# Turned attention probabilities kept in DRAM in another order: four stores a unit for two, one load for four

## The chip, the cores and the metric

The kernel runs on one core of a Trainium2 chip. The metric is the device time of one execution in microseconds (us), the median of several runs. The core has a matrix engine (PE, with its weight loads shown as PEld), a vector engine (DVE), a scalar engine (ACT), a general engine (POOL), and SP, which computes nothing and only issues transfers (DMAs). Each engine works through its own list of instructions in order and waits on semaphores. Transfers are issued here by SP and by ACT and are moved by 16 DMA engines that both share.

## The reference

Sparse causal attention over 8 batches, 8 heads, 576 positions and 64 features, followed by a feed-forward layer over all 4608 tokens. All of it is float32.

```python
scores = scale * np.matmul(q, k.transpose(0, 1, 3, 2))
rel = pos[:, None] - pos[None, :]
mask_local = (rel >= 0) & (rel < stride)                    # stride 32, heads 0 to 3
mask_strided = (rel >= 0) & (pos[None, :] % stride == pos[:, None] % stride)   # heads 4 to 7
...
attn = np.exp(scores)
attn = attn / (np.sum(attn, axis=-1, keepdims=True) + 1e-09)
return np.matmul(attn, v).astype(np.float32)
...
h = x @ w_in                                                # 4608x512 by 512x2048
g = np.where(pos, h, np.where(neg, 0.0, (h + beta) ** 2 / (4.0 * beta)))
return (g @ w_out).astype(np.float32)                       # 4608x2048 by 2048x512
```

## The kernel before

**Two kinds of work share PE.** The feed-forward layer is most of it: nine chunks of 512 tokens. The first three are computed plainly (`up`, L775, and `down`, L820, 16 slices of the hidden layer each). The other six are taken in three pairs by a scheme with seven products for eight (`up_block`, L917, and `down_block`, L1005). Each float32 operand is split into two rounded parts, so a product takes three matmuls. The weights of the seven-product part are sums of weight blocks that are kept in DRAM (`kq`, `ks`). SP fetches them with `fetch_w` (L845) into a ring of seven tiles `wr`: as soon as PE is done with one tile, the transfer for the tile seven places later may go.

**Attention feeds the layer.** A batch is four units: 0 and 1 hold the local heads, 2 and 3 the strided heads. Units 0 and 2 have n = 6 slots, unit 1 has 3 and unit 3 has 5. A slot holds, on 128 partitions, four groups of 32 queries, against 64 keys for each of two heads. For each unit: scores on PE (L482), mask, maximum, exponential, sum and division on DVE, ACT and POOL, then the turn of the probabilities from "query on the partitions" to "key on the partitions", and last the value step on PE (`value`, L669), which multiplies them with V into `xp`. Its result is copied into the feed-forward input.

**The turn has two forms.** Batches 0 and 1 turn on PE (`flip`, `keep`). Batches 2 to 7, that is 24 units, do it in three steps. `turn` (L633) transposes 32x32 blocks on DVE, into two tiles `t`, one for each head h, whose partition is (group i, key c within its half) and whose row is (half of the keys k, slot n, query q). `spread` (L643) stores the two tiles to a DRAM tile `there`. `gather` (L654) loads it back into `pT`, whose partition is (head h, half k, key c) and whose row is (group i, slot n, query q), which is what the value step reads. PE runs the value steps of units 1 and 3 of a batch together (`values_1_3`).

**What sets the order.** All is issued in an order written out by hand: the table `WORK` gives each step of each unit a place between the matmul groups of the feed-forward layer (`s` scores, `t` turn, `j` spread, `J` gather, `v` and `V` value). SP's list holds, in that order, the loads of q, k and v, the stores and loads of `there`, the fetches of `wr`, and the output. A load of `there` waits until the stores have landed, and SP issues nothing behind it until then. SP's transfers take turns on eight semaphores; a transfer whose semaphore is still in use waits for the one that uses it.

The turn and the two steps that the change touches:

Of the kernel before, what the change touches and what calls it, by code (L numbers as in the profile page):

```python
# [8 lines left out]
F32 = mybir.dt.float32  # L9
# [8 lines left out]
P = 128  # L18
EPS = 1e-09
ST = 32  # L20
# [153 lines left out]
def tile_sparse_attention_then_ffn(  # L174
# [14 lines left out]
    nc = tc.nc  # L189
    B, _, _, _, S = qk_l.shape  # L190
# [27 lines left out]
    def slots(u):  # L218

        n, rest = divmod(UNITS[u][2], IL if UNITS[u][0] else IS)  # L220
        return n + (rest > 0), n
# [18 lines left out]
    dram = ctx.enter_context(tc.tile_pool(name="dram", bufs=1, space=bass.MemoryType.DRAM))  # L240
# [31 lines left out]
    for i in range(IL):  # L272
        part = slice(i * QL, (i + 1) * QL)
        for n0, n1, off in ((0, SLOTS, ST),) if i else ((0, 1, 0), (1, SLOTS, ST)):
            t = m_loc[part, n0:n1]
# [4 lines left out]
    for i in range(IS):  # L280
        t = m_str[i * QS:(i + 1) * QS]
# [164 lines left out]
    def attention(b, kinds):  # L446

        probs, flipped, there, ahead, covered = {}, {}, {}, {}, set()
# [188 lines left out]
        def spread(u):  # L637

            ts = probs.pop(u)
            n = sum(slots(u))  # L640
            there[u] = to = dram.tile([P, 2, 2, n, ST], F32, tag=f"t{u}", name=f"there_{b}_{u}")
            for h in range(2):
                nc.sync.dma_start(to[:, h], ts[h][:, :, :n])  # L643

        def gather(u):

            n = sum(slots(u))
            pool, tag = (o_p, "ob") if u == 1 else (pt_p, "pT")
            pT = pool.tile([P, 4, n if u == 1 else 2 * SLOTS, ST], F32, tag=tag, name=f"pT_{b}_{u}")
            src = there.pop(u).rearrange("(i c) h k n q -> h k c i (n q)", c=ST)  # L650
            for h in range(2):
                for k in range(2):
                    at = h * 64 + k * ST
                    nc.sync.dma_start(pT[at:at + ST, :, :n].rearrange("p i n q -> p i (n q)"), src[h, k])  # L654
            flipped[u] = pT

        def value(u, xp=None):
# [85 lines left out]
        def in_two(do, rest):  # L743

            return lambda u: do(u, rest if b == 0 else None)

        steps = {"s": score, "y": score_0, "z": score_1, "m": mask, "o": opened, "i": cover, "g": plain, "X": most_there, "S": below_there, "x": most, "w": norm_v, "a": below_max, "e": expo, "q": total, "p": plus_eps, "k": plus_eps_v, "b": below_max_v, "r": norm,
                 "f": flip, "t": turn, "j": spread, "J": gather, "c": keep, "d": keep_v, "v": value, "V": values_1_3, "h": in_two(high, False), "l": in_two(low, False), "H": in_two(high, True), "M": in_two(low, True),
                 "Q": lambda p: fetch_qk(b, p), "P": lambda n: last_weights(n), "F": lambda n: fetch_v(b, ((0, 0), (0, 1), (1, 0), (2, 0), (3, 0))[n])}
        def go(names):  # L750
# [292 lines left out]
    with tc.manual_schedule():  # L1043
# [33 lines left out]
        for s, work in G_WORK.items():  # L1077
            for t, name in work:
                m, k = int(name[1]), int(name[2:])
# [13 lines left out]
        for c in range(CLASSIC):  # L1093
            for f in range(NF):
                t = 4 * (NF * (c - 1) + f)
# [17 lines left out]
        for s in range(NSC):  # L1113
            t = 4 * NF * (CLASSIC - 1) + 2 * len(UP) * s
# [61 lines left out]
```

## Time and profile before

| | us |
|---|---|
| median of three runs | 816.55 (816.5 to 817.0) |
| the profiled execution | 817.29 |
| its span | 815.5 |
| PE busy | 806.2 |
| DVE, ACT, POOL busy | 574.7, 495.4, 232.5 |

The profile is of one execution. Its span runs from the first to the last instruction; the execution's own time also holds what lies around it, 1.8 us. A page gives the busy time of each engine, the DMA queues (q1 is SP's, q10 is ACT's) and the chain of work that ended last, followed back from the end. Rows of a timeline give start, length, engine, line, operation, what is written from what, and how often. Rows on DMA issues give how many, the size of each, and the median time from issue to landing. In the trace the three plain chunks end at about 328 us, the first store of `there` is issued at 135.6 us and the last load of it at 559 us.

### The profile page before, as it was taken

How to read it: one execution, taken by the hardware profiler on the slowest of the kernel's cores; microseconds unless marked ns; L12 is line 12 of the kernel's file. 1: busy time of each engine (PE TensorE's matmuls, PEld its weight loads, DVE VectorE, ACT ScalarE, POOL GpSimd, SP SyncE). 2: the span in 40 equal slices, each digit the busy share in tenths (PEclk: the TensorE clock that was granted, in tenths of full speed). 3: DMA queues.
4: the chain of work that ended last, by engine and by line, in shares of the span. 5: the costliest groups of instructions: out<-in, count | busy, mean ns of one | idle time of the engine just before them, and what ended most of it. 6: DMA issues, size and time to landing. Idle time of an engine off the chain costs nothing.

```text
span 815.5 us, 17861 instructions
## 1 busy us (share of the span) xinstructions
PE 806.2 (99%) x6969; PEld 656.9 (81%) x6969; DVE 574.7 (70%) x850; ACT 495.4 (61%) x866; POOL 232.5 (29%) x226
## 2 busy tenths in 40 slices
PE   8999999999999999999999999999999999999998
PEld 6788888878878888887878888888888888888886
DVE  5898868767548477776778876675589834558664
ACT  5888955545355365776775453778654647775442
POOL 5353544873347543023222000220120001114100
PEclk9999999999999999999999999999999999999999
DMA  9936437788868867987998768887666776666765
GB/s 344 408 138 201 153 111 274 265 298 278 265 221 299 286 243 257 304 287 247 285 288 266 216 203 249 263 265 228 193 193 213 232 235 196 196 192 190 216 200 170
DMA packets 101796, 195.10 MB, mean 239 GB/s; under 512 B 17105, under 2 KB 32465, under 8 KB 99665
## 3 DMA queue, kind: packets, MB, share of 16 engines
q1 hardware_dynamic: 92496, 164.60, 63.3%
q10 hardware_dynamic: 9216, 29.36, 9.4%
q8 instruction: 55, 0.90, 0.5%
q14 instruction: 29, 0.23, 0.1%
HBM read 147.26 MB, written 46.66 MB: 238 GB/s over the span
## 4 chain that ended last, share of the span: by engine, by line
PE 91%; DMA 5%; issue 1%; DVE 1%; ACT 1%; POOL 0%; SPq 0%; ACTq 0%; POOLq 0%
PE o L820 16%; PE h L775 16%; PE yo L1005 15%; PE y L917 15%; PE zo L1005 8%; PE z L917 7%; PE xo L1005 4%; PE x L917 4%; PE xp L669 3%; PE sc L482 3%; DMA wr<-kq 1%; DMA qk<-in_qk_s 1%; DMA there<-t 1%; DMA pT<-there 1%; DMA qk<-in_qk_l 1%
## 5 line engine op out<-in xcount | busy, mean ns | idle before, releaser
L917 PE MATMUL y<-x,wr 128*128 128x512 f32 x576 | 141.3, 392 | 0.0
L775 PE MATMUL h<-xq,w 128*128 128x512 f32 x576 | 140.0, 392 | 0.1
L1005 PE MATMUL yo<-hl,wr 128*128 128x512 f32 x576 | 132.8, 390 | 0.6 <-DMA wr<-kq 0.6
L820 PE MATMUL o<-gh,w 128*128 128x512 f32 x384 | 130.1, 399 | 0.0
L1005 PEld LDWEIGHTS yo<-hl,wr 128*128 128x128 f32 x576 | 108.0, 188 | 23.4 <-DMA wr<-kq 1.0
L775 PEld LDWEIGHTS h<-xq,w 128*128 128x128 f32 x576 | 107.4, 188 | 23.4 <-DVE xq L739 0.7
L917 PEld LDWEIGHTS y<-x,wr 128*128 128x128 f32 x576 | 107.4, 188 | 22.7
L820 PEld LDWEIGHTS o<-gh,w 128*128 128x128 f32 x384 | 72.1, 188 | 16.2
L820 PE MATMUL o<-gl,w 128*128 128x512 f32 x192 | 75.0, 391 | 0.0
L917 PE MATMUL z<-x,wr 128*128 128x512 f32 x288 | 73.7, 391 | 0.0
L957 POOL TENSOR_TENSOR ga<-gb,ga 128x1024 f32<-128x1024 f32 x9 | 21.6, 2397 | 167.5 <-DVE ga L785 141.7
L1005 PE MATMUL zo<-hl,wr 128*128 128x512 f32 x288 | 66.1, 390 | 0.0
L572 POOL TENSOR_TENSOR pr<-pr,st 128x384 f32<-128x384 f32 (+3 forms) x21 | 26.3, 1253 | 135.7 <-DVE st L595 64.5
L1005 PEld LDWEIGHTS zo<-hl,wr 128*128 128x128 f32 x288 | 54.0, 188 | 11.3
L917 PEld LDWEIGHTS z<-x,wr 128*128 128x128 f32 x288 | 53.8, 188 | 11.3
L782 ACT ACTIVATE tmp<-tmp 128x512 f32<-128x512 f32 x96 | 60.7, 632 | 3.0
L871 DVE TENSOR_TENSOR hl<-ga,hl 128x1024 fp32r<-128x1024 f32 x36 | 47.3, 1315 | 19.9 <-ACT hl L870 18.2
L870 ACT CAST hl<-ga 128x1024 fp32r<-128x1024 f32 x36 | 38.0, 1056 | 35.1 <-PE yo L1005 12.6
L396 POOL TENSOR_TENSOR xs<-w 128x512 f32<-128x512 f32 x32 | 45.1, 1426 | 48.4 <-DMA ks<-xs 32.8
L785 DVE SCALAR_TENSOR_TENSOR h<-h,u 128x512 f32<-128x512 f32 x47 | 32.8, 697 | 30.5 <-ACT u L782 30.1
L398 POOL TENSOR_TENSOR xs<-xs 128x256 f32<-128x256 f32 x64 | 51.3, 802 | 5.0
L779 ACT ACTIVATE u<-h,half 128x512 f32<-128x512 f32 x48 | 33.1, 689 | 29.6 <-PE h L775 24.1
(120 smaller groups left out, 1321.9 us busy)
## 6 DMA issues: line engine op xcount, KB each, us to landing
wr<-ks SPq DMA_DIRECT2D x192, 256.0 KB, 3.9
wr<-kq SPq DMA_DIRECT2D x144, 256.0 KB, 3.4
ks<-xs ACTq DMA_DIRECT2D x16, 1024.0 KB, 4.8
raw<-in_w SPq DMA_DIRECT2D x30, 512.0 KB, 9.6
kq<-w ACTq DMA_DIRECT2D x48, 256.0 KB, 3.8
qk<-in_qk_s SPq DMA_DIRECT2D x16, 604.0 KB, 6.1
qk<-in_qk_l SPq DMA_DIRECT2D x16, 576.0 KB, 6.0
v<-in_v_l SPq DMA_DIRECT2D x21, 384.0 KB, 6.0
```

What stands on the lines that cost most here:

```text
L396: nc.gpsimd.tensor_tensor(out=b[:, :, f] if i else b[:, f], in0=hi, in1=lo, op=ALU.add)
L398: nc.gpsimd.tensor_tensor(out=st[:, to, HF:], in0=st[:, x, HF:], in1=st[:, y, HF:], op=op)
L572: eng.tensor_tensor(out=pr, in0=pr, in1=st[:, 0].unsqueeze(2).broadcast_to(list(pr.shape)), op=ALU.add)
L775: nc.tensor.matmul(o_ps[c, f], wt[f][:, 0, h, x, e:e + P], xq[c][:, y, cc], start=first and n == 0, stop=last and n == len(todo) - 1)
L779: nc.scalar.activation(u, h, AF.Relu, bias=half, scale=0.5)
L782: nc.scalar.activation(u, u, AF.Square)
L785: nc.vector.scalar_tensor_tensor(out=to, in0=h, scalar=1.0, in1=u, op0=ALU.max, op1=ALU.min)
L820: nc.tensor.matmul(o_ps[c][d], wt[f][:, 1, h, x, e:e + P], gs[y], start=f == 0 and n == 0, stop=f == NF - 1 and n == 2)
L870: nc.scalar.copy(t[:, 0], src)
L871: nc.vector.tensor_tensor(out=t[:, 1], in0=src, in1=t[:, 0].bitcast(F32), op=ALU.subtract)
L917: nc.tensor.matmul(to, w_[:, a, c * P:(c + 1) * P], xc[m][:, b, c], start=m in (1, 2, 5) and c + q == 0, stop=c == 1 and q == 2, skip_grou ...
L1005: nc.tensor.matmul(to, w_[jj][:, a, d * P:(d + 1) * P], t[:, b, jj], start=m in (1, 2, 5) and k + jj + q == 0, stop=k == NP // 2 - 1 and j ...
```

## The change

The DRAM tile is laid out as (group, head, half, key, slot, query). Before, it was (partition, head, half, slot, query), where the partition is group and key together. The bytes are the same.

```diff
-            there[u] = to = dram.tile([P, 2, 2, n, ST], F32, tag=f"t{u}", name=f"there_{b}_{u}")
+            there[u] = to = dram.tile([4, 2, 2, ST, n, ST], F32, tag=f"t{u}", name=f"there_{b}_{u}")
             for h in range(2):
-                nc.sync.dma_start(to[:, h], ts[h][:, :, :n])
+                for k in range(2):
+                    nc.sync.dma_start(to[:, h, k], ts[h][:, k, :n])
...
-            src = there.pop(u).rearrange("(i c) h k n q -> h k c i (n q)", c=ST)
-            for h in range(2):
-                for k in range(2):
-                    at = h * 64 + k * ST
-                    nc.sync.dma_start(pT[at:at + ST, :, :n].rearrange("p i n q -> p i (n q)"), src[h, k])
+            src = there.pop(u).rearrange("i h k c n q -> (h k c) i (n q)")
+            nc.sync.dma_start(pT[:, :, :n].rearrange("p i n q -> p i (n q)"), src)
```

Two stores of a unit become four, one for each head and half of the keys. On the DRAM side a store now walks four groups, in each 32 keys that follow each other, in each a row of n x 32 floats. Four loads of 32 partitions become one of 128, whose DRAM side walks 128 rows (head, half, key) and in each four groups. Of all engines' lists only SP's changes. Its order shows it at two places. The first is unit 0 of batch 2, the first that is turned this way, and the start of unit 1. A row names the line, what is written from what (names carry batch and unit), the shape of the written side, and how many equal rows follow each other. Before:

```order
L810 DMA out_0<-xs_0_1874 128x512 x4
L643 DMA there_2_0_2011<-t_2_0_0_2007 128x384
L643 DMA there_2_0_2011<-t_2_0_1_2009 128x384
L654 DMA pT_2_0_2027<-there_2_0_2011 32x4x192 x4
L431 DMA v_2_1_0_2218<-in_v_l 128x768
L643 DMA there_2_1_2220<-t_2_1_0_2151 128x2x96
L643 DMA there_2_1_2220<-t_2_1_1_2153 128x2x96
L654 DMA pT_2_1_2276<-there_2_1_2220 32x4x96 x4
```

The same place of the changed kernel:

```order
L808 DMA out_0<-xs_0_1874 128x512 x4
L644 DMA there_2_0_2011<-t_2_0_0_2007 4x32x192 x2
L644 DMA there_2_0_2011<-t_2_0_1_2009 4x32x192 x2
L652 DMA pT_2_0_2029<-there_2_0_2011 128x4x192
L431 DMA v_2_1_0_2217<-in_v_l 128x768
L644 DMA there_2_1_2219<-t_2_1_0_2150 4x32x96 x2
L644 DMA there_2_1_2219<-t_2_1_1_2152 4x32x96 x2
L652 DMA pT_2_1_2277<-there_2_1_2219 128x4x96
```

The steps stand at their old places; each store has become two with a written side of 4x32 rows, and the four loads have become one. The second place is unit 2 of batch 7 on SP, where fetches of `wr` stand between its stores and its loads. Before:

```order
L643 DMA there_7_2_6775<-t_7_2_0_6749 128x384
L643 DMA there_7_2_6775<-t_7_2_1_6751 128x384
L845 DMA wr_140_6784<-ks_0_3_156 128x512
L845 DMA wr_141_6798<-ks_0_4_158 128x512
L845 DMA wr_142_6810<-kq_0_3_155 128x512
L431 DMA v_7_2_0_6815<-in_v_s 128x768
L845 DMA wr_143_6824<-ks_0_4_158 128x512
L654 DMA pT_7_2_6828<-there_7_2_6775 32x4x192 x4
L845 DMA wr_144_6842<-kq_0_5_159 128x512
L845 DMA wr_145_6851<-ks_0_4_158 128x512
```

The same place of the changed kernel:

```order
L644 DMA there_7_2_6753<-t_7_2_0_6727 4x32x192 x2
L644 DMA there_7_2_6753<-t_7_2_1_6729 4x32x192 x2
L843 DMA wr_140_6764<-ks_0_3_156 128x512
L843 DMA wr_141_6778<-ks_0_4_158 128x512
L843 DMA wr_142_6790<-kq_0_3_155 128x512
L431 DMA v_7_2_0_6795<-in_v_s 128x768
L843 DMA wr_143_6804<-ks_0_4_158 128x512
L652 DMA pT_7_2_6808<-there_7_2_6753 128x4x192
L843 DMA wr_144_6819<-kq_0_5_159 128x512
L843 DMA wr_145_6828<-ks_0_4_158 128x512
```

Four fetches and a load of V still stand between the stores and the load of `pT`, and the next fetches still stand behind it.

## The prediction

> **What bounds the kernel now.** I read the page first: span, engine shares, DMA queues, chain by engine and the DMA issues.
>
> ```profile
> span 815.5 us, 17861 instructions
> ...
> PE 806.2 (99%) x6969; PEld 656.9 (81%) x6969; DVE 574.7 (70%) x850; ACT 495.4 (61%) x866; POOL 232.5 (29%) x226
> ...
> q1 hardware_dynamic: 92496, 164.60, 63.3%
> q10 hardware_dynamic: 9216, 29.36, 9.4%
> ...
> PE 91%; DMA 5%; issue 1%; DVE 1%; ACT 1%; POOL 0%; SPq 0%; ACTq 0%; POOLq 0%
> ...
> ks<-xs ACTq DMA_DIRECT2D x16, 1024.0 KB, 4.8
> ...
> kq<-w ACTq DMA_DIRECT2D x48, 256.0 KB, 3.8
> ```
>
> PE is busy for 99% of the span, and the change touches none of its instructions. So the change can help only by removing a wait of PE, and can hurt only by making one. How much there is to remove stands in the busy times by stage (window, then its length and the busy PE; near the row's end the clock, the DMA share and GB/s):
>
> ```profile
> 127.00:227.00 100.00, 99.78 (x1030) 81.12 (x1029) 69.83 (x122) 48.82 (x91) 55.20 (x57) 1.00 0.80 278
> 227.00:318.00 91.00, 91.00 (x1085) 73.61 (x1084) 56.87 (x92) 47.71 (x97) 49.39 (x50) 1.00 0.74 257
> 318.00:430.00 112.00, 111.13 (x1122) 89.72 (x1121) 83.26 (x131) 78.07 (x145) 24.82 (x20) 1.00 0.89 285
> 430.00:505.00 75.00, 75.00 (x546) 61.69 (x546) 57.42 (x54) 38.58 (x52) 3.75 (x2) 1.00 0.77 233
> 505.00:570.00 65.00, 64.86 (x591) 52.99 (x582) 43.58 (x77) 47.81 (x92) 10.80 (x10) 1.00 0.82 250
> ```
>
> All 24 changed units lie between 127 and 570 us, where PE idles 0.22 + 0.87 + 0.14 = 1.2 us: the most that can be won, 0.15% of the time. The clock is 1.00 throughout. From 318 us on, when the ring of seven tiles `wr` must be fed as well, the DMA engines are 82 to 89% busy wherever units are stored. The chain of waits shows how such a unit stands to PE (start, us, what):
>
> ```profile
> 532.22 0.76 DVE t L633 x2
> 532.98 5.95 DMA there<-t
> ...
> 539.00 0.32 SPq L654
> ...
> 540.46 5.94 DMA pT<-there
> 546.40 0.14 issue
> 546.53 0.92 PE xp L669 x44
> ```
>
> Turn, store (5.95 us to landing), four loads issued over 1.46 us, landing 5.94 us after the last issue, and PE's value step starts 0.1 us later. PE lost nothing here, but **nothing was to spare** either. The waits of PE and of SP's queue say the same (total, times, longest):
>
> ```profile
> PE yo L1005 <- DMA wr<-kq: 0.6, 1, 0.6
> ...
> SPq L654 <- DMA there<-t: 38.1, 19, 4.3
> ```
>
> In 19 of 24 units SP stands at the first load until the stores have landed, with everything behind it, the fetches of `wr` too. And PE has already waited once, 0.6 us, for such a fetch.
>
> **The change, part by part.** These are the transfers concerned:
>
> ```profile
> there<-t SPq DMA_DIRECT2D x24, 192.0 KB, 5.3
> pT<-there SPq DMA_DIRECT2D x48, 96.0 KB, 3.8
> ...
> there<-t SPq DMA_DIRECT2D x12, 160.0 KB, 3.2
> ...
> there<-t SPq DMA_DIRECT2D x12, 96.0 KB, 4.1
> ```
>
> Bytes stay. Stores go from 48 to 96 issues and loads from 96 to 24, so SP issues 24 DMAs fewer. By the chain's four issues in 1.46 us from first to last (0.49 each) that is 24 x 0.49 = 12 us less on SP in all. SP is no bound, and the cover is PE's own work, so I cost it at nothing, beyond what it does for one unit's latency, below.
>
> *The load.* Before, the last of four quarter loads leaves 1.46 us after the first; now one transfer leaves at once and carries all the data. For the data's time I use the rate of one engine under this kernel's traffic: q1's 63.3% of 16 x 815.5 us is 8,259 us of engine time for 164.60 MB, 19.9 KB per us. A unit of 384 KB (two stores of 192 KB, 393,216 bytes) then takes 1.23 us on 16 engines, and a quarter 0.31 us. So the load ends 1.46 + 0.31 - 1.23 = 0.5 us earlier.
>
> *The stores.* Here lies the risk. In the order's rows a store's DRAM side was 128x384 and is now 4x32x192: group, key, data, with a jump between groups. The DRAM side of a store therefore counts four at its outermost step, where that of every transfer before counted 32 or more. What the trace shows of dealing out is this. ACT's queue moved 16 + 48 = 64 transfers of 128 rows, 8,192 rows; it recorded 9,216 packets, so 1,024 are left over: 16 small ones for each, one for every engine. No row shows a transfer whose outermost step counts fewer than 16. If one is cut along that step, a store has four shares for four engines, and the other twelve stand by. Bounds for a 384 KB unit: on 16 engines the data takes 1.23 us as before; on four, 393,216 / 4 / 19.9 = 4.9 us. At q10's rate (9.4% of 13,048 us for 29.36 MB, 23.9 KB per us) it is 4.1 us on four.
>
> I take four engines. All the rows show is that a transfer with 128 outer steps reaches sixteen engines; for sixteen the chip would have to look past the outermost step, and nothing in the trace says that it does. [...]
>
> What a unit pays: before, the second store left 0.49 us after the first and had 0.62 us of data, so data ended 1.1 us after the first issue. Now four issues (about 1.9 us) hide behind 4.9 us of data on four engines. That is +3.8 us, at the faster rate 4.1 - (0.49 + 0.51) = +3.1 us; I take 3.5. With the load's -0.5 a 384 KB unit's probabilities arrive **3.0 us later**. A 320 KB unit scales by 5/6 in its data: store +2.9, load -0.7, net 2.2. The 192 KB unit is not waited for alone: its value step runs with the fourth unit's.
>
> Who pays: nine value steps stand from 318 us on, three in each of the last three batches. The first and the last of the nine, each by its store, the store's landing, its loads, their landing, and PE:
>
> ```profile
> 318.35 1.25 SPq L643 DMA_DIRECT2D there<-t  x2
> ...
> there<-t SPq DMA_DIRECT2D x2, 192.0 KB, 5.3
> ...
> 332.54 1.85 SPq L654 DMA_DIRECT2D pT<-there  x4
> ...
> pT<-there SPq DMA_DIRECT2D x4, 96.0 KB, 5.0
> ...
> 339.64 1.60 PE L669 MATMUL xp<-pT,v 64*64 64x32 f32 x96
> ...
> 549.48 0.90 SPq L643 DMA_DIRECT2D there<-t  x2
> ...
> there<-t SPq DMA_DIRECT2D x2, 160.0 KB, 3.2
> ...
> 557.60 1.85 SPq L654 DMA_DIRECT2D pT<-there  x4
> ...
> pT<-there SPq DMA_DIRECT2D x4, 80.0 KB, 3.7
> ...
> 562.56 1.51 PE L669 MATMUL xp<-pT,v 64*64 64x32 f32 x88
> ```
>
> Loads land about 0.7 us ahead of PE at the first (332.5 + 1.4 + 5.0 = 339.0) and as much at the last (562.7; the fourth unit's part starts after 48 of the 88, at 563.4); in the chain's unit 0.1. I take 0.5 as the mean. At these two, however, the loads start 8 and 4 us after their stores landed, so a store 3 us later costs nothing. Seven steps are left: five of 384 KB and two of 320 KB, 5 x (3.0 - 0.5) + 2 x (2.2 - 0.5) = 15.9 us. The stage ahead has nine more steps, of which the first reads:
>
> ```profile
> 141.61 1.75 SPq L654 DMA_DIRECT2D pT<-there  x4
> ...
> pT<-there SPq DMA_DIRECT2D x4, 96.0 KB, 2.5
> ...
> 146.10 1.60 PE L669 MATMUL xp<-pT,v 64*64 64x32 f32 x96
> ```
>
> 141.6 + 1.3 + 2.5 = 145.4 against 146.1: 0.7 to spare, so 3.0 - 0.7 = 2.3 us. The other eight I cost at nothing: no `wr` is fetched there until 323 us, so a late SP harms only the value step itself.
>
> *The fetches behind.* SP stands up to 3.5 us longer at a load, and fetches queue behind the stores' backlog on the four engines. When PE waits for the value step, they win the same time, so I add nothing in the likeliest case. Without that cover each of the 12 units after 318 us could cost the whole 3.5 us: 42 us, the upper end.
>
> Sum: 15.9 + 2.3 = 18.2 us on the profiled execution's 817.3 us (span 815.5 and 1.8 around it), 835.5. The median is 816.55, 0.7 below that execution, so I say **835 us**.
>
> **The rivals.**
>
> *Sixteen engines after all (not slower).* Place: the cut of a store on the way to DRAM. The four issues end at 1.46 us, plus 0.31 us of data: 1.8 against 1.1 before, +0.7, which the load's -0.5 nearly takes back. PE sees nothing, or wins part of its 1.2 us: 815.4 to 817, likely 816.3. It decides from about eight engines on: the data then takes 2.5 us, a unit comes 0.9 us late and little passes the 0.5 us to spare. For it: every transfer of the trace ran so, loads included whose DRAM side steps over four groups inside. Against it: those count 32 outside.
>
> *Four engines, mostly hidden.* If the other traffic rarely meets the four engines and PE's first waits give the later units their time back, only the three tightest steps pay, 3 x 2.5 = 7 us: 820 to 826, likely 824. For it: stores are a small part of the bytes. Against it: each unit's chain starts from PE's progress again, so one stall does not prepay the next.
>
> *Four engines that clog.* Seven units lie in 318 to 430 us: four of 384 KB at +3.7 us of engine time, two of 192 KB at +1.85, one of 320 KB at +3.1, 21.6 us. On engines busy 0.89 of 112 us (99.7) this makes 121 us, 9 us over the stage's length before any latency, and every fetch has its share on these engines. With the fetch term at half to full, 20 to 40 us: 840 to 858, likely 848.
>
> **How the numbers follow.** Forecast (827 to 840) 0.60, clogged 0.17, mostly hidden 0.13, sixteen engines 0.10. What this kernel's measurement can tell from no change is about 0.2%, 1.6 us. A gain above that exceeds PE's 1.2 us of idle time: faster 0.02; same 0.08, nearly all of the sixteen-engine case; slower 0.90. The range leaves out the sixteen engines (0.10), a sliver of the hidden case below 820 (0.02) and the end of the clogged one above 852 (0.07): 820 to 852.
>
> **What would show it.** The packets of q1 decide the engines: a unit's stores and load make 512 + 512 data packets now, with 16 small ones for the load and 4 or 16 for each of four stores. Against today's 92,496 that gives 94,032 on four engines and 95,184 on sixteen. Landing of the stores should rise from 5.3 to 8 or 9 us with 3.5 us more of SP waiting at the load, the load's own landing be below 1.46 + 3.8 us from the first issue, and PE show waits for `pT` of 2 to 3 us at about seven value steps after 340 us, with 318 to 430 us the most stretched stage. I am wrong if q1 shows sixteen engines, or if PE's new waits name `wr` rather than `pT`.

## The result, and the profile after

The changed kernel takes **852.0 us** (850.3 to 853.0) against 816.8 us before (816.5 to 817.0): a ratio of 1.042, with an interval of 1.039 to 1.045. That is 35 us slower. The forecast was slower, 835 us, with a range of 820 to 852. The direction and the four engines were right; the loss is twice the 18 us that I had added up, and 852.0 lies at the very end of the range. The page of the changed kernel, with the row of the granted clock in 40 slices among it:

```profile
span 850.0 us, 17804 instructions
...
PE 817.4 (96%) x6969; PEld 663.3 (78%) x6969; DVE 573.3 (67%) x850; ACT 496.3 (58%) x866; POOL 230.9 (27%) x226
...
PEclk9999999798999989999999999999999999999999
...
q1 hardware_dynamic: 94032, 164.59, 59.6%
q10 hardware_dynamic: 9216, 29.36, 9.3%
...
PE 75%; DMA 18%; DVE 2%; issue 2%; SPq 1%; ACT 1%; POOL 1%; DVEq 0%; POOLq 0%; ACTq 0%
```

q1 recorded 94,032 packets, to the packet the number for stores on four engines; sixteen would have given 95,184. DMA's share of the chain grew from 5% to 18%. The span is 34.5 us longer, in two parts: PE idles 850.0 - 817.4 = 32.6 us where it idled 9.3, so 23.3 more; and PE is busy for 11.2 us more with the same 6,969 matmuls, since the granted clock is no longer full everywhere.

Where it went stands in the busy times of the three parts with the same work: batches 2 to 4 up to their last value step, batches 5 to 7 likewise, and the rest. After:

```profile
127.00:336.00 209.00, 190.16 (x2034) 153.87 (x2033) 120.60 (x203) 91.66 (x172) 98.04 (x101) 0.94 0.69 236
336.00:600.00 264.00, 258.10 (x2309) 207.56 (x2308) 187.33 (x268) 167.01 (x292) 44.09 (x35) 1.00 0.78 254
600.00:850.00 250.00, 246.31 (x1087) 203.58 (x1085) 163.22 (x169) 140.69 (x197) 29.57 (x11) 1.00 0.65 201
```

Before, the same three parts:

```profile
127.00:308.00 181.00, 180.78 (x2026) 146.71 (x2025) 120.21 (x202) 89.81 (x170) 99.35 (x101) 1.00 0.78 271
308.00:565.00 257.00, 255.99 (x2307) 208.28 (x2307) 188.17 (x268) 166.29 (x292) 44.34 (x35) 1.00 0.84 261
565.00:815.00 250.00, 246.83 (x1089) 204.13 (x1087) 163.26 (x169) 141.21 (x198) 29.87 (x11) 1.00 0.65 201
```

The first part is 28 us longer: PE idles 18.8 us there for 0.2, and the clock is 0.94. The second is 7 us longer, with 5.9 us of idle time for 1.0. I had put 15.9 us into the second part and 2.3 into the first. The waits of PE and SP by releaser (total, times, longest):

```profile
PE xp L667 <- DMA pT<-there: 14.7, 7, 5.4
PE xp L667 <- issue: 6.5, 2, 5.9
...
SPq L652 <- DMA there<-t: 87.7, 37, 8.0
```

PE waits at the value step, as forecast, but three waits carry most of it. They are in PE's timeline, the wait in brackets at the end: unit 0 of batch 2, unit 2 of batch 2 and unit 2 of batch 4.

```profile
153.52 2.78 PE L667 MATMUL xp<-pT,v 64*64 64x32 f32 x96 [5.92 <-issue]
...
193.41 1.67 PE L667 MATMUL xp<-pT,v 54*64 54x64 f32 x48 [5.40 <-DMA pT<-there]
...
315.61 1.56 PE L667 MATMUL xp<-pT,v 54*64 54x64 f32 x48 [5.42 <-DMA pT<-there]
```

At the first the profile names no releaser; the load of `pT` was issued at 149.1 us and is what the step needs. PE had gone idle at 147.6, 188.0 and 310.2 us; 2.1, 2.6 and 3.3 us later the clock falls to half, and stays there for 6.8 to 10.2 us (window, length and busy PE; clock, DMA share and GB/s at the end):

```profile
149.70:159.90 10.20, 6.38 (x105) 5.57 (x106) 4.77 (x9) 3.46 (x6) 5.56 (x7) 0.50 0.61 204
190.60:197.40 6.80, 3.99 (x54) 3.42 (x55) 2.00 (x3) 3.21 (x7) 0.00 (x0) 0.50 0.43 159
313.50:320.30 6.80, 4.69 (x56) 3.93 (x57) 3.07 (x7) 2.12 (x7) 5.45 (x6) 0.50 0.58 193
```

PE works 6.38 + 3.99 + 4.69 = 15.1 us at the half clock, where the matmuls of L818 start 0.43 us apart, for 0.23 at the full one; I estimate the loss from the clock, at about 7.5 us. With 16.7 us of waiting, **three value steps cost about 24 us of the 35**. Some 2 us of the busy time are not the change's: this execution had a half clock for 3.5 us at 20 us as well, before the first store.

### The profile page after: what moved, and what is told of

Read it like the earlier page. It is cut to its first block, busy times and chain, and to the rows that moved or that the text cites. A ratio compares the mean times of both kernels' runs of the same rounds, so it can differ in the third digit from the quotient of the medians.

```text
span 850.0 us, 17804 instructions
## 1 busy us (share of the span) xinstructions
PE 817.4 (96%) x6969; PEld 663.3 (78%) x6969; DVE 573.3 (67%) x850; ACT 496.3 (58%) x866; POOL 230.9 (27%) x226
## 3 DMA queue, kind: packets, MB, share of 16 engines
q1 hardware_dynamic: 94032, 164.59, 59.6%
## 4 chain that ended last, share of the span: by engine, by line
PE 75%; DMA 18%; DVE 2%; issue 2%; SPq 1%; ACT 1%; POOL 1%; DVEq 0%; POOLq 0%; ACTq 0%
PE yo L1003 14%; PE y L915 12%; PE h L773 11%; PE o L818 11%; PE zo L1003 8%; PE z L915 6%; DMA there<-t 5%; PE xo L1003 4%; PE xp L667 3%; DMA wr<-kq 3%; PE x L915 3%; PE sc L482 3%; DMA pT<-there 3%; DMA qk<-in_qk_s 2%; DMA qk<-in_qk_l 1%
## 5 line engine op out<-in xcount | busy, mean ns | idle before, releaser
L818 PE MATMUL o<-gh,w 128*128 128x512 f32 x384 | 132.0, 404 | 0.0
L818 PEld LDWEIGHTS o<-gh,w 128*128 128x128 f32 x384 | 73.5, 191 | 16.9
L818 PE MATMUL o<-gl,w 128*128 128x512 f32 x192 | 76.1, 396 | 0.0
L667 PE MATMUL xp<-pT,v 64*64 64x32 f32 (+2 forms) x1760 | 34.6, 230 | 21.7 <-DMA pT<-there 14.7
```

Of the source, the lines that this page charges most:

```text
L667: nc.tensor.matmul(xp[p][j * D:(j + 1) * D, n], loaded[b, local, b0 + n][keys, j], qs, start=True, stop=True)
L818: nc.tensor.matmul(o_ps[c][d], wt[f][:, 1, h, x, e:e + P], gs[y], start=f == 0 and n == 0, stop=f == NF - 1 and n == 2)
```

## The experiments

Each difference is against the kernel before, run on the same chip beside it (817.0 to 817.7 us), unless another is named.

**1. Four engines without the rest of the change.** The kernel before, with a gap behind each group of the DRAM tile. Units 0 and 2 keep their two stores; units 1 and 3, whose rows in `t` do not fill the tile and so have a gap between the two halves of the keys, take four.

```diff
-there[u] = to = dram.tile([P, 2, 2, n, ST], F32, ...)
+there[u] = to = dram.tile([4, ST + 1, 2, 2, n, ST], F32, ...)
...
-                nc.sync.dma_start(to[:, h], ts[h][:, :, :n])
+                if n == 2 * SLOTS:
+                    nc.sync.dma_start(to[:, :ST, h], ts[h][:, :, :n])
+                else:
+                    for k in range(2):
+                        nc.sync.dma_start(to[:, :ST, h, k], ts[h][:, k, :n])
```

> The kernel before, with 32 unused rows' worth of one gap behind each group of the DRAM tile, so that its stores count four at the outermost step; the loads are the four of before, and units 0 and 2 keep two stores of 192 KB (units 1 and 3 take four). Theory 'four engines' (the cut along the outermost step costs the time): slower than before by 25 to 45 us, 842 to 862 us, and q1 loses 12 small packets for each store. Rival 'more and smaller stores' or 'the one load': units 0 and 2 have neither, so within 5 us of 816.8.

The gap is one row of the tile behind each group (`ST + 1`), not the 32 rows that this text speaks of. Measured: 855.6 us, ratio 1.047 (1.043 to 1.051). Its page's q1 and its waits of PE:

```profile
q1 hardware_dynamic: 92016, 164.60, 59.6%
```

```profile
PE xp L673 <- DMA pT<-there: 11.7, 9, 4.2
```

The packets are 480 fewer than before: 12 for each of 24 stores in units 0 and 2, and 16 a unit in the other twelve, which now have 4 x 132 for 2 x 272. So these stores ran on four engines too, and the loss, 38 us, is about that of the changed kernel with four loads (experiment 3, 39 us). A gap of one row per group is enough.

**2. Four stores, on sixteen engines.**

```diff
-there[u] = to = dram.tile([P, 2, 2, n, ST], F32, ...)
+there[u] = to = dram.tile([2, 2, P, n, ST], F32, ...)
...
-                nc.sync.dma_start(to[:, h], ts[h][:, :, :n])
+                for k in range(2):
+                    nc.sync.dma_start(to[h, k], ts[h][:, k, :n])
...
-src = there.pop(u).rearrange("(i c) h k n q -> h k c i (n q)", c=ST)
+src = there.pop(u).rearrange("h k (i c) n q -> h k c i (n q)", c=ST)
```

> Four stores a unit as in the change, but into a DRAM tile (head, half, group, key), where each store is 128 rows behind each other and counts 128 at the outermost step; four loads as before. Theory 'four engines': 816 to 819 us, since every store has sixteen engines again and doubling the stores costs only 0.5 us of issuing each. Rival 'more and smaller stores': most of the 35 us stay, above 835 us.

Measured: 821.3 us, ratio 1.003 (1.001 to 1.005). Its q1:

```profile
q1 hardware_dynamic: 96336, 164.60, 63.2%
```

The packets are 3,840 more than before, as they are with 16 small ones for each of the 96 stores; with four it would be 95,184. Twice as many stores, each half as large, cost 2.6 us (1 to 4), above the 816 to 819 us that I expected, and a small part of the 35.

**3. The one load taken apart again.** The changed kernel with four loads.

```diff
-            src = there.pop(u).rearrange("i h k c n q -> (h k c) i (n q)")
-            nc.sync.dma_start(pT[:, :, :n].rearrange("p i n q -> p i (n q)"), src)
+            src = there.pop(u).rearrange("i h k c n q -> h k c i (n q)")
+            for h in range(2):
+                for k in range(2):
+                    at = h * 64 + k * ST
+                    nc.sync.dma_start(pT[at:at + ST, :, :n].rearrange("p i n q -> p i (n q)"), src[h, k])
```

> The changed kernel with its one load taken apart into the four loads of 32 partitions of before; the stores stay on four engines. If the one load is worth the 0.5 us a unit of the prediction, paid where PE waits: 854 to 858 us (852 + 7 to 10 waits x 0.5). If it is worth 1.5 to 2 us a unit, as issue to landing in the two traces suggests, 862 to 872 us. If the load is worth nothing, 852.

Measured: 856.7 us, ratio 1.049 (1.046 to 1.052), against the changed kernel's 1.042 (1.039 to 1.045): the one load is worth about 0.7%, some 5 us, as the first of the three cases says. The two intervals only just lie apart. So here one load of 128 partitions does better than four on quarters of them, and what puts the stores on four engines weighs some seven times as much (38 us in experiment 1).

**4. PE kept busy at the three waits.** Dummy matmuls of zeros in front of the three value steps, through the kernel's own step `Z`.

```diff
-(17.04, 'v0')
+(17.04, 'Zv0:50 v0')
...
-(37.36, 'v2')
+(37.36, 'Zv2:46 v2')
...
-(107.04, 'v2')
+(107.04, 'Zv2:46 v2')
```

> The changed kernel with dummy matmuls of zeros (50, 46 and 46, about 0.1 us each) put before the value step of units 0 and 2 of batch 2 and of unit 2 of batch 4, where PE waited 5.9, 5.4 and 5.4 us and the granted clock fell to a half for 10.2, 6.8 and 6.8 us. The results are written over by the value step. Theory 'idle PE lowers the clock': no half clock at these places, PE's busy time without the dummies 7 us less, 843 to 848 us. Rival 'the clock falls for another reason': half clock stays, 850 to 853 us.

Measured: 844.6 us (839.7 to 852.0), ratio 1.034 (1.029 to 1.038), some 7 us below the changed kernel. The three places in the profiled execution, clock third from the end:

```profile
140.00:160.00 20.00, 20.00 (x240) 16.49 (x238) 10.49 (x17) 7.83 (x13) 13.61 (x16) 1.00 0.68 225
180.00:200.00 20.00, 18.10 (x191) 14.62 (x190) 11.54 (x19) 7.95 (x14) 7.36 (x8) 1.00 0.57 196
300.00:320.00 20.00, 19.48 (x190) 15.88 (x192) 11.28 (x15) 11.24 (x19) 6.69 (x7) 1.00 0.54 173
```

The half clock is gone, so at these places it was PE's idling that brought it. The times of this kernel scatter by 12 us, and its profiled execution was the slowest: PE works 809.1 us there without the 16.3 of the dummies, 8.3 less than in the changed kernel's, but other waits took this back (from 336 to 600 us PE idles 13.4 us for 5.9). So the 7 us agree with the 7.5 worked out above but do not measure them closely. In the changed kernel's trace the half clock had come 2.1 to 3.3 us into the waits.

**5. The change by batches.** The changed code under a condition, the old code otherwise: `b < 5` in one kernel, `b > 4` in the other.

> The change in batches 2 to 4 alone; batches 5 to 7 as before. By the two traces, value steps up to the last of batch 4 are 26 to 28 us late and the rest adds 6 to 7: 842 to 846 us. By the prediction's split (15.9 us in the late batches, 2.3 in the early ones): 819 to 822 us.

> The change in batches 5 to 7 alone; batches 2 to 4 as before. By the two traces 822 to 825 us; by the prediction's split 832 to 835 us. With the run of the early batches the two losses should add up to about 35 us.

Measured: 842.3 us for batches 2 to 4 (ratio 1.033, 1.029 to 1.036) and 826.1 us for batches 5 to 7 (1.011, 1.008 to 1.014): 25.3 and 9.1 us, together 34.4. The losses add up, and my split of 2.3 and 15.9 was wrong. The late batches came out 1 us above the 822 to 825 expected. PE's waits in the kernel with these alone:

```profile
PE yo L1016 <- DMA wr<-kq: 2.2, 2, 1.9
PE yo L1016 <- DMA wr<-ks: 1.5, 2, 0.9
...
PE xp L680 <- DMA pT<-there: 0.9, 2, 0.5
```

So in its profiled execution PE waits more for the fetches of `wr` than at the value step.

**6. The change in three units alone.** The condition is now `(b, u) in ((2, 0), (2, 2), (4, 2))`.

> The change in three units alone, before whose value steps PE waited longest in the changed kernel: units 0 and 2 of batch 2 and unit 2 of batch 4; the other 21 units as before. Theory 'three units carry most': each 5.4 to 5.9 us of waiting and 2 to 3 us of half clock, 24 us in all: 836 to 842 us. Rival 'the late stores hold up SP's list and the loss builds up over many units': below 830 us.

Measured: 839.1 us, ratio 1.028 (1.024 to 1.032), 22 us. PE's waits and the half clock stand where they stood:

```profile
PE xp L680 <- DMA pT<-there: 10.5, 2, 5.4
PE xp L680 <- issue: 6.4, 2, 5.4
```

```profile
151.50:158.40 6.90, 6.22 (x104) 5.49 (x105) 2.94 (x8) 1.35 (x3) 5.02 (x7) 0.51 0.52 178
189.10:195.90 6.80, 4.19 (x54) 3.62 (x55) 2.06 (x4) 3.15 (x7) 0.00 (x0) 0.50 0.52 174
308.60:315.40 6.80, 4.46 (x55) 3.79 (x56) 2.55 (x4) 1.77 (x5) 5.20 (x6) 0.50 0.76 250
```

Three units of 24 make nearly two thirds of the loss. Nothing had to build up over many units.

**7. Shorter packets on ACT's queue.** From 127 to 318 us before, the engines' time is shared like this by SP's queue and ACT's:

```profile
q1 hardware_dynamic: 17086, 23.53, 39.3%
q10 hardware_dynamic: 8496, 27.27, 37.2%
```

ACT's 1 MB transfers go in packets of 8 KB, 2,048 for the 16 of them. My theory was that a store's small packet takes turns with one of these, so that shorter ones would let the stores through.

```diff
-        nc.scalar.dma_start(kept[i][j][1].rearrange("p n x e -> p n (x e)"), st)
+        nc.scalar.dma_start(kept[i][j][1].rearrange("p n x e -> p n (x e)"), st, max_dma_last_dim=2048)
```

> The changed kernel with the 1 MB transfers of ACT's queue (ks) cut into rows of 2 KB for 8 KB; bytes and number of transfers stay. Theory 'packet for packet': on the four engines a small packet of a store takes turns with one packet of ACT's queue, so with packets a quarter as long the stores of batches 2 to 4 land some us earlier; the waits of 5.4 to 5.9 us before three value steps shrink, and 835 to 847 us. Rival 'the load of the engines counts, not the packet': within 2 us of the changed kernel, 850 to 853 us.

The same edit in the kernel before:

> The kernel before with the same cut of ACT's 1 MB transfers into 2 KB rows. Both theories: no wait of PE hangs on them there, 816 to 818 us.

Measured: 852.7 us, ratio 1.044 (1.041 to 1.046), as without the edit, and 818.0 us for the control, 1.001 (0.999 to 1.003). The packets of the 1 MB transfers did become four times as many and a quarter as long, so that q10 has 6,144 more:

```profile
q10 hardware_dynamic: 15360, 29.36, 9.9%
```

That theory falls: the size of ACT's packets does not decide.

**8. Without ACT's transfers.** The feed-forward weights are then not those of the reference: only the first pair's tiles are stored, and every fetch reads these.

```diff
-        nc.scalar.dma_start(kept[i][j][1].rearrange("p n x e -> p n (x e)"), st)
+        if (i, j) == (0, 0):
+            nc.scalar.dma_start(kept[i][j][1].rearrange("p n x e -> p n (x e)"), st)
...
-            if n != (1, 0):
+            if n != (1, 0) and (i, j) == (0, 0):
...
-            nc.sync.dma_start(ring[n].bitcast(F32), kept[i][j][which][:, at])
+            nc.sync.dma_start(ring[n].bitcast(F32), kept[0][0][which][:, at])
```

> The kernel before without nearly all of ACT's transfers (the weight sums and copies kq and ks are stored for the first pair of slices alone, and every fetch of wr reads that pair's tiles; so the feed-forward result is not the reference's). All theories: within 3 us of the kernel before, 814 to 819 us, since PE hardly waits there.

> The changed kernel with the same transfers of ACT left out. Theory 'ACT's traffic on the four engines makes the early stage dear' (127 to 318 us: q10 has 37% of the engines' time): the waits of 5.4 to 5.9 us before the value steps of batches 2 and 4 shrink below 2 us, no half clock follows them, and 824 to 834 us. Rival 'the four engines alone are as slow without other traffic': 845 us or more.

Measured: 817.5 us for the kernel before so cut (1.000, 0.998 to 1.002), and 827.5 us for the changed one (1.014, 1.009 to 1.019): of the 35 us 10 are left, about what batches 5 to 7 cost alone. PE in the first two windows, and its waits, of the changed kernel so cut:

```profile
127.00:336.00 209.00, 207.78 (x2232) 168.46 (x2231) 141.60 (x232) 107.18 (x202) 109.97 (x108) 1.00 0.43 137
336.00:600.00 264.00, 256.92 (x2216) 207.09 (x2215) 181.07 (x259) 169.28 (x295) 41.94 (x29) 1.00 0.75 245
```

```profile
PE xp L668 <- DMA pT<-there: 2.9, 4, 1.2
```

Up to 336 us PE idles 1.2 us for 18.8 and the clock is full. The packets of q1 are still 94,032, so the stores still go to four engines; what made the early ones so slow is ACT's traffic beside them, in whatever packets. That the two meet on the four engines fits this, but no run tells it from their meeting in DRAM.

## Why the prediction was right in kind and half in size

**Nothing to gain, PE as the bound: right.** PE idled 1.2 us over the changed stretch, and no run came out below the kernel before by more than its interval.

**Four engines: right.** The packet count decided it, and experiment 1 shows that it suffices. That a store is cut along its outermost step was my estimate; no transfer of the trace before could show it. In the packet records of that trace q1 has 9,936 packets of 4 bytes, 16 for each of SP's 621 transfers; in the changed kernel's it has 8,400, as many as 16 for each of 501 transfers and 4 for each of the 96 stores. From 145.2 to 147.9 us, while unit 0's stores run with little beside them (q1 takes 16.3% of the sixteen engines' time, q10 8.1%), the changed kernel's DMA view (40 slices, tenths of all sixteen engines busy) shows mostly one to three tenths, about the quarter that four engines make:

```profile
DMA  2223223233132931121411111132222322211111
```

In the trace's packet records the 512 data packets of these four stores run at most six at a time; of the 256 of the same unit's two stores before, up to nineteen overlap.

**The rival of more issues: small.** Doubling the stores costs 2.6 us; I had 0.7 us a unit, to be made good by the load.

**A unit 3.0 us late: mis-sized both ways.** This is the term that failed. It came from one rate for all engines and the whole span, 19.9 KB per us. In the early stage the stores run beside ACT's traffic. SP's timeline shows unit 2 of batch 2, before and then changed:

```profile
162.75 1.24 SPq L643 DMA_DIRECT2D there<-t  x2
166.97 3.56 SPq L654 DMA_DIRECT2D pT<-there  x4
```

```profile
172.87 4.28 SPq L644 DMA_DIRECT2D there<-t  x4
187.17 0.38 SPq L652 DMA_DIRECT2D pT<-there  x1
```

From the first store to the load it takes 14.3 us for 4.2. Unit 0 of batch 2 takes 12.1 for 6.0 and unit 2 of batch 4 9.4 for 3.6: 6 to 10 us more, where I had 3.5. The chain through unit 2 of batch 2 in the changed kernel:

```profile
176.08 11.01 DMA there<-t
...
187.17 6.00 DMA pT<-there
193.17 0.25 issue
193.41 1.67 PE xp L667 x46
```

The last store takes 11 us to land, where I had 4.9 us of data and the median before was 5.3. In the late stage the unit whose chain the prediction shows reads, stores from SP's timeline first:

```profile
567.22 2.44 SPq L644 DMA_DIRECT2D there<-t  x4
```

```profile
569.00 6.43 DMA there<-t
575.43 0.02 issue
575.45 5.35 DMA pT<-there
580.80 0.14 issue
580.94 0.93 PE xp L667 x48
```

From its first store to its load it takes 8.2 us for 6.0 before (+2.2, I had +3.5), and from the load to landing 5.35 us for 539.00 to 546.40, 7.4 (-2.05, I had -0.5). So the value step starts 13.7 us after the first store, where it was 13.6, and PE waits 0.42 us in place of 2.5. In this unit the one load gains four times what I gave it; experiment 3 prices it at some 5 us for the whole kernel. SP's waiting at the load rose from 38.1 / 24 = 1.6 us a unit to 87.7 / 24 = 3.7 (37 waits for 24 loads), by 2.1 and not 3.5.

**"The other eight I cost at nothing": wrong.** I reasoned that no fetch of `wr` stands behind a late unit there. True, and the value step itself waited: batches 2 to 4 cost 25 us. I had read the time to spare for none of the eight. Before, unit 2 of batch 2 had some 2 to 3 us (its loads, issued up to 170.5 us, took 4.9 us at the median to land, and its value step began at 177.8): about what I thought a unit would lose, but it came 10 us later to its load.

**"The clock is 1.00 throughout": true before, and no term of the sum.** I priced a wait by its length. Each of the three long ones also brought a half clock behind it, under which PE worked 4.0 to 6.4 us and so, by the estimate above, lost some 2 to 3.

**The fetches: part of the late loss.** I added nothing for them and put 15.9 us on seven waits for `pT` of 2 to 3 us. From 336 to 600 us the changed kernel has four waits for `pT`, together 2.9 us and the longest 1.1, and PE's waits for `wr` sum to 2.0 of its 5.9 us of idle time. In the kernel with the late batches alone they are 4.0 of 6.0 us, and those for `pT` 0.9. So the late batches lose 7 to 9 us, and only in part at the step that I named.

**The range: held by luck.** The early batches lost 23 us more than I had put there and the late ones 7 less, and the sum fell on the end of the range. The rival "four engines that clog" (840 to 858) has the number but not the place: it looked for the loss from 318 to 430 us, and most of it lies ahead of that.

## What to carry to other kernels

Before a DRAM tile is laid out anew for the load's sake, look at the store's DRAM side: here stores of 128 rows at even distances ran on sixteen engines, those of four groups of 32 rows with a gap between the groups on four, and a gap of one row was enough. Count a queue's packets: here the small ones that come with each transfer, 16 or 4, told the two apart. Price a transfer on few engines by what else is moved in that stage (a last store took 11.0 us to land, where a mean over the span had given 4.9 us of data), not by a mean over the span; and price a wait of PE of some 5 us with the slower clock that follows it (here a half for 6.8 to 10.2 us). Read the time to spare at every step that a late transfer can hold up, also where nothing else queues behind it.

## What the runs showed of the hardware that I had not expected

A wait of PE of 5.4 to 5.9 us brought a half clock of 6.8 to 10.2 us, which began while PE still waited: at 149.7 us for a wait that ended at 153.5. Shorter waits could do it too. In experiment 3 none of PE's waits at the value step was longer than 3.2 us, and the clock was at half for 10.2 us about the step of unit 0 of batch 2, with PE idle for 2.5 of them:

```profile
PE xp L670 <- DMA pT<-there: 11.0, 10, 2.7
PE xp L670 <- issue: 3.9, 2, 3.2
```

```profile
148.70:158.90 10.20, 7.69 (x107) 6.58 (x108) 5.41 (x9) 2.99 (x6) 5.55 (x7) 0.50 0.61 212
```

In experiment 4 PE's longest wait, 2.5 us, brought none: the mean granted clock of that execution is 1.0.

```profile
PE yo L1003 <- DMA wr<-kq: 2.8, 2, 2.5
```

What decides is not shown. In the changed kernel's trace the half clocks that ended before the run did lasted 3.4, 6.8, 6.8 and 10.2 us.

SP also took longer to issue a store of the changed kernel, 0.51 us at the median, than one of before with twice the bytes, 0.38 us. And cutting ACT's packets to a quarter changed neither kernel's time, although leaving ACT's transfers out took away 25 of the 35 us.
